# Mixed tiles of a top-k attention scaled on ScalarE and GpSimd instead of VectorE, and a re-ordered schedule

## The chip, the cores and the metric

The kernel runs on one core of a Trainium2 chip. The metric is the device time of one execution in microseconds (us), as the median of several runs.

## The reference

The reference is attention that keeps, for each query, the 32 largest of 576 scores, followed by a feed-forward block whose activation is a rational function:

```python
scores = (1 / sqrt(D)) * q @ k.transpose(0, 1, 3, 2)      # batch 8, heads 8, seq 576, D 64
kth = np.partition(scores, -32, axis=-1)[..., -32:-31]
scores = np.where(scores >= kth, scores, -1e9)
attn = exp(scores - max(scores))
attn = attn / (sum(attn) + 1e-9)
x = (attn @ v), heads side by side                        # 4608 tokens x 512
h = x @ w_in                                              # 512 -> 2048
P = a[0] + a[1]*h + a[2]*h**2 + a[3]*h**3
Q = 1 + abs(b[0])*abs(h) + abs(b[1])*h**2
out = (P / (Q + 1e-6)) @ w_out                            # 2048 -> 512
```

All data are fp32.

## The kernel before

**Tiles.** Heads are taken in pairs (hp, four pairs per batch). The 576 queries of a head are four blocks of 128 and a tail of 64. A *tile* is one head's block of 128 queries against all 576 keys; a *mixed tile* holds the 64-query tails of both heads of a pair, the one on partitions 0 to 63, the other on 64 to 127. There are 288 tiles in 160 units: 128 units of two tiles, and 32 mixed units of one.

**One tile.** TensorE makes the scores s (L570; L567 for a mixed tile), ScalarE copies them to SBUF as sb (L577). VectorE finds the 32nd largest value by folding (L596) and by rounds of MAX8 and MATCH_REPLACE8 (L602, L613, L621). GpSimd makes st, the negated maximum, ScalarE the exponentials e (L675), and VectorE the masked probabilities pr with their row sums ss (L678). The reciprocal of ss is spread over 64 columns per head as rw (`widen`, on GpSimd or ScalarE).

**One unit.** TensorE turns pr (`transpose`, L773) into a PSUM bank trp and, with the last block of keys, also rw (L775); ScalarE evacuates these as p0, p1, p2 (L785). p2 holds the last block of probabilities and, beside it, the turned reciprocals. TensorE multiplies with the values (av, L799). `scale` then multiplies av with the reciprocals. In an ordinary unit ScalarE copies av to x (L816) and GpSimd multiplies (L818). In a mixed unit VectorE does two products of 64 partitions by 64 columns, one per head (L826), into xm, which a DMA stores in xtail; the four batches of one tail chunk are fetched from there.

**Feed-forward.** The attention's output is taken in 18 chunks of 256 tokens. A chunk is split into high and low fp32r parts (xh, xl) and goes through eight groups: hidden layer (ph, 24 matmuls, L940), the rational function on ScalarE, GpSimd and VectorE (L952 to L1028), and the output product po (L1100, or L1107 for groups with split weights).

**Weights.** They come as 64-bit floating point numbers, are put together on ScalarE (L390, L401, L405), VectorE (L395) and GpSimd (L409), and are split into high and low parts (L274 on ScalarE or L276 on GpSimd, then L431) in the first 200 us, beside the attention. The keys are split the same way (L274 or L276, then L485 on GpSimd).

**The order.** All steps are entered in a list with an estimated length, a key (priority), what they depend on, and the buffers that they take and give (`add`). A planner (`Plan.run`) walks through an imagined time: an engine that is free takes the ready step with the lowest key, and a step that several engines can do goes to the first that is free. The instructions are issued in the order in which the planner starts them, and each engine runs its own in that order. The estimated lengths (`dve`, `act`, `pool_t`, ...) and the numbers in `KEY` so decide the order and the engine of every step. Buffers are rings of a few slots: two PSUM banks "mm" for trp, av and ph, one "s" for scores, one p2.

```python
bh = Hold("mm")
x = add("PE", n * pe_t, transpose(i), dep, kk, take=[bh] + ([] if at else [thold[i]]))
ev.append(add("ACT", act(n * P), evacuate(i), [x], kk + KEY['URG'], give=[bh]))
```

A second pass over everything (`full`), for data on which folding loses a value, stands behind a branch and isn't run here.

Of the kernel before, what the change touches and what calls it, by code (L numbers as in the profile page):

```python
# [10 lines left out]
F32 = mybir.dt.float32  # L11
# [6 lines left out]
AX = mybir.AxisListType  # L18
PSUM = bass.MemoryType.PSUM

KEY = {'LN': 12, 'UV': 'DVE', 'UK': -499.369, 'B0': ('ACT',), 'B1': ('POOL', 'DVE'), 'B2': ('DVE', 'POOL'), 'B3': ('DVE', 'POOL'), 'WH': ('POOL', 'ACT'), 'XH': ('POOL', 'ACT'), 'TH': 0, 'EU': -5.754, 'HW': 256, 'Q0': ('POOL', 'ACT'), 'Q1': ('POOL',), 'SPLIT': (0, 2, 4, 6), 'XS': 1, 'RH': ('ACT',), 'p2': ('POOL',), 'p4': ('POOL',), 'ratio': ('POOL',), 'ratio_low': ('POOL',), 'URG': -104.067, 'PT': -8.421, 'AV': -16.325, 'MOE': 55.665, 'LOOK': 0.27, 'T': 5.775, 'KL': -0.464, 'PJ': 35.19, 'WL': -13.886, 'EX': 43.184, 'EW': 12.91, 'ALT': {'ACT': 0.094, 'DVE': 95.307, 'POOL': 1.524}, 'WG': 4.177, 'QL': -6.4, 'PACE': 11.206, 'MS': -0.749, 'NM': ('POOL',), 'WD': ('POOL', 'ACT'), 'LP': ('POOL',), 'VL': -14.255}
NEG = -3.0e38
NB = 8

# [154 lines left out]
def tile_topk_attention__then__rational_ffn(  # L179
# [48 lines left out]
    def add(*args, **kwargs):  # L228
        return plan.add(*args, **kwargs)
# [17 lines left out]
    act = lambda n, ptr=0: 0.06 + n / 1200 + 0.094 * ptr  # L247
    act_sb = lambda n, ptr=0: act(n, ptr) + 0.04
    pool_s = lambda n, ptr=0: 0.16 + n * 0.00084 + 0.083 * ptr
    pool_t = lambda n: 0.15 + n * 0.0021  # L250
    pe_r = lambda n: max(0.109, n / 2230 + 0.003)
    pe_f = lambda n: 2 * max(0.109, n / 1200 + 0.003)
    pe_t = 0.109
# [9 lines left out]
        return {e: f[e] for e in engs}  # L263

    def fused(n, *engs):
        f = {"POOL": pool_s(n, 1) + pool_t(n), "DVE": 0.069 + n / 420}
        return {e: f[e] for e in engs}

    def engine():
# [78 lines left out]
    def weight_block(src, r0, e0, split, key, nm):  # L348
# [21 lines left out]
        else:  # L370
# [12 lines left out]
            for i in range(2):  # L383

                def low(i=i):
                    es, low, high = o.parts[i]
                    if i == 0:
                        o.bits = bank(xhold, [P, 512], f"wb_{nm}")
                        o.w = words(0) if lo is not None else hi if plain else hi(F32)
                    nc.scalar.activation(o.bits[:, es], low.bitcast(U32), AF.Identity, scale=STEP, bias=two_)  # L390

                def high(i=i):
                    es, low, high = o.parts[i]
                    x = o.bits[:, es].bitcast(I32)
# [12 lines left out]
                def join(i=i):
                    es, low, high = o.parts[i]
                    nc.gpsimd.tensor_tensor(  # L409
                        out=o.w[:, es], in0=o.w[:, es], in1=high.bitcast(F32), op=ALU.mult  # L410
                    )

                s1 = add("ACT", act(256), low, [ld] + first, key + 1,
                         take=[] if first else [xhold] + (hold if lo is not None else []))
                first = [s1]
                s2 = add("DVE", dve(256), high, [s1], key + 1)
                s3 = add("ACT", act_sb(256), sign, [s2], key + 1)
                s4 = add("ACT", act(256), size, [s2], key + 2, give=[xhold])
# [130 lines left out]
    def add_tile(t):  # L549
# [173 lines left out]
        else:  # L723
# [2 lines left out]
            a_ = add("DVE", dve(TH), best(1), [a_], key + 0.02)  # L726
            a_ = add("DVE", 0.055 + dve(TH), less(1), [a_], key + 0.04)
            a_ = add("DVE", dve(XW), best(2), [a_, b0_, b1_], key + 0.045)
            a_ = add("DVE", 0.055 + dve(XW), less(2), [a_], key + 0.046, give=[hihold])
            kb = add("DVE", dve(XW), best(3), [a_], key + 0.047)  # L730
            u.tops += [kb]
        if not full and t is u.last:
# [2 lines left out]
            u.batch.over.append(o_)  # L735
            if len(u.batch.over) == HP * NJ + HP:
                add("DVE", 0.15, worst_of(u.bi, u.batch), u.batch.over, key + 0.1, give=[u.batch.hold])
        t.probs = add("DVE", 0.06 + dve(S), probs, [kb, ex], key + 0.2, give=[sbhold, mhold, ehold])


    def add_values(u):
# [22 lines left out]
        def transpose(i):  # L764
            def emit():
# [5 lines left out]
                    cols = [slice(MAIN, MAIN + P)]  # L771
                for c, x in enumerate(cols):
                    nc.tensor.transpose(u.ps[i][:, c * P : (c + 1) * P], u.pr[:, x], ident)  # L773
                if i == 2:
                    nc.tensor.transpose(  # L775
                        u.ps[i][:, P : 2 * P], u.rw.rearrange("p h d -> p (h d)"), ident
                    )
            return emit

        def evacuate(i):  # L780
            def emit():
                n = NJ if i < 2 else 2
                if pair.pT[i] is None:
                    pair.pT[i] = buf(thold[i], [P, 2, n, P], F32, f"p{i}_{u.nm}")
                nc.scalar.copy(  # L785
                    pair.pT[i][:, at].rearrange("p c n -> p (c n)"), u.ps[i][:, 0 : n * P]
                )
            return emit

# [16 lines left out]
        def scale(part=0):  # L806
# [14 lines left out]
                return  # L821
            if not hasattr(u.batch, "xm"):
                u.batch.xm = buf("xm", [P, HP, TAIL], F32, f"xm_{u.bi}")
            for h in range(2):
                d = slice(h * D, (h + 1) * D)
                nc.vector.tensor_tensor(u.batch.xm[d, u.hp], pair.av[d, 0:TAIL], rb[d, 0, d], ALU.mult)  # L826


        def put():
            nc.sync.dma_start(u.chunk.away[:, :, u.x0 : u.x0 + TAIL], u.batch.xm)  # L830
# [7 lines left out]
        for i in ([0, 2] if u.mixed else [0, 1, 2]):  # L838
# [5 lines left out]
            bh = Hold("mm")  # L844
            n = NJ if i < 2 else 2
            kk = KEY['PT'] + (u.tiles[0].key + T if i == 0 else key + 0.4 * i)
            x = add("PE", n * pe_t, transpose(i), dep, kk, take=[bh] + ([] if at else [thold[i]]))
            tp.append(x)
            x.give = [u.phold]
            if i == 2:  # L850
                x.give = [u.phold, rwhold]
            ev.append(add("ACT", act(n * P), evacuate(i), [x], kk + KEY['URG'], give=[bh]))
            if not at:
                pair.first[i] = ev[-1]
        u.phold.users = len(tp)
# [1 line left out]
        if u is not pair.units[-1]:  # L857
            return
        avh = Hold("mm")
        n_av = 1.4 * pe_t if u.mixed else 2.7 * pe_t if lone else 4.1 * pe_t  # L860
        m = None
        cuts = [[0, 1, 2], [3, 4]] if u.mixed or lone else [[0, 1], [2, 3], [4]]
        for cs in cuts:
            m = add("PE", len(cs) * n_av, multiply(cs), [m] if m else pair.ev + [pair.vload], key + KEY['AV'],
                    take=[] if m else [avh] + ([] if u.chunk.parts or u.mixed else [u.chunk.hold]))
        m.give = [pair.vhold] + [thold[0]] + ([] if u.mixed else [thold[1]])
        m2, n = m, u.nq * len(pair.units)
# [6 lines left out]
                give=[avh, thold[2]],  # L874
            )
        else:
            s = add(
                "DVE", 2 * dve(TAIL), scale, [m2] + u.batch.xs[0:1], key + KEY['URG'],
                take=[] if u.batch.xs else [u.batch.xmhold], give=[avh, thold[2]],
            )  # L880
            u.batch.xs.append(s)
            if len(u.batch.xs) < HP:
                return
# [443 lines left out]
```

## Time and profile before

| | |
|---|---|
| median of 3 runs | 1557.52 us (1556.35 to 1557.78) |
| profiled execution: device time | 1558.06 us |
| profiled execution: span from first to last instruction | 1556.3 us |
| mean granted TensorE clock, as a share of 2.4 GHz | 0.971 |

PE is TensorE's matmuls, PEld its weight loads, DVE is VectorE, ACT ScalarE, POOL GpSimd. Busy time is the union of an engine's instructions. A matmul's duration includes its way through the array, so matmuls in a row overlap: how fast they follow each other is read from a group of several.

### The profile page before, as it was taken

The numbers are of one execution on the slowest core, as the hardware profiler recorded it, in microseconds if no ns is written. First come the engines' busy times: TensorE is split into PE (matmuls) and PEld (weight loads), VectorE is DVE, ScalarE is ACT, GpSimd is POOL, SyncE is SP. The second block draws the span as 40 slices with busy tenths as digits, with TensorE's granted clock in tenths as the row PEclk, the third lists the DMA queues.
The fourth block names the chain that finished last, engine by engine and source line by source line (L and its number), as shares of the span: only waits on it lengthen the run. The fifth ranks groups of instructions, "written<-read, shape, count | busy, mean of one in ns | idle before, by whom it ended". The sixth has DMA issues, their size and how long they took to land.

```text
span 1556.3 us, 31312 instructions
## 1 busy us (share of the span) xinstructions
PE 1431.3 (92%) x9441; PEld 1115.2 (72%) x9441; DVE 1391.3 (89%) x5541; ACT 1351.4 (87%) x2542; POOL 1155.5 (74%) x1619
## 2 busy tenths in 40 slices
PE   2447899999999999999999999999999999999996
PEld 1235666867776778777788877787787778788774
DVE  6888999999999899499999999999999989799742
ACT  6888997989898898899999998999897988798873
POOL 7877885768666795869877886688787897788520
PEclk9668999999999999999999999999999999999998
DMA  7634433233422243223422243224422333121111
GB/s 236 235 107 127 130 107 100 59 87 91 132 71 74 76 123 108 63 66 89 131 84 78 74 135 100 79 57 119 122 76 75 95 101 100 57 66 51 48 46 52
DMA packets 86802, 148.93 MB, mean 96 GB/s; under 512 B 12640, under 2 KB 38240, under 8 KB 86624
## 3 DMA queue, kind: packets, MB, share of 16 engines
q1 hardware_dynamic: 86560, 146.83, 31.5%
q8 instruction: 77, 1.26, 0.3%
q14 instruction: 101, 0.83, 0.2%
q0 software_dynamic: 64, 0.00, 0.1%
HBM read 134.22 MB, written 12.58 MB: 94 GB/s over the span
## 4 chain that ended last, share of the span: by engine, by line
PE 75%; ACT 9%; DVE 6%; POOL 4%; DMA 3%; issue 2%; SPq 1%; POOLq 0%; ACTq 0%; DVEq 0%
PE ph_m L940 20%; PE po_m L1100 12%; PE po_m L1107 11%; PE av L799 10%; PE trp L773 8%; PE s L570 7%; PE ph_t L940 3%; PE s L567 2%; ACT p L785 2%; PE po_t L1100 1%; DVE m L613 1%; PE po_t L1107 1%; ACT sb L577 1%; ACT e L675 1%; DMA out_dram<-ob_m 1%
## 5 line engine op out<-in xcount | busy, mean ns | idle before, releaser
L940 PE MATMUL ph_m<-xh_m,win_h 128*128 128x256 f32 x1024 | 314.5, 307 | 9.1 <-ACT p L785 8.5
L613 DVE MAX8 m<-x 128x8 f32<-128x192 f32 (+1 forms) x864 | 308.0, 356 | 3.4
L940 PE MATMUL ph_m<-xh_m,win_l 128*128 128x256 f32 x1024 | 287.8, 281 | 0.0
L940 PE MATMUL ph_m<-xl_m,win_h 128*128 128x256 f32 x1024 | 287.7, 281 | 0.0
L773 PE MATMUL trp<-ident,pr 128*128 128x128 f32 x1312 | 224.4, 281 | 52.1 <-ACT wout L405 17.3
L785 ACT COPY p<-trp 128x512 f32<-128x512 f32 (+1 forms) x448 | 231.2, 520 | 28.6 <-PE trp L773 20.1
L1100 PE MATMUL po_m<-wout,pa_m 128*128 128x512 f32 x512 | 247.9, 595 | 0.7 <-POOL pa_m L994 0.7
L773 PEld LDWEIGHTS trp<-ident,pr 128*128 128x128 f32 x1312 | 161.6, 143 | 119.9 <-ACT p L785 27.6
L570 PE MATMUL s<-k,q 128*128 128x288 f32 x1024 | 208.4, 327 | 37.7 <-DVE x L596 17.5
L596 DVE TENSOR_TENSOR pr<-s,sb 128x192 f32<-128x192 f32 x576 | 197.9, 345 | 49.4 <-PE trp L773 31.3
L675 ACT ACTIVATE e<-sb,st 128x576 f32<-128x576 f32 x288 | 219.2, 761 | 19.4 <-POOL st L282 14.6
L678 DVE SCALAR_TENSOR_TENSOR pr<-sb,m,e 128x576 f32<-128x576 f32 x288 | 230.2, 799 | 4.7 <-ACT e L675 2.1
L577 ACT COPY sb<-s 128x576 f32<-128x576 f32 x288 | 186.5, 647 | 50.7 <-PE s L570 37.0
L940 PEld LDWEIGHTS ph_m<-xh_m,win_h 128*128 128x128 f32 x1024 | 194.7, 190 | 27.2 <-ACT p L785 14.8
L570 PEld LDWEIGHTS s<-k,q 128*128 128x128 f32 x1024 | 154.8, 196 | 76.7 <-POOL k L485 14.0
L940 PEld LDWEIGHTS ph_m<-xl_m,win_h 128*128 128x128 f32 x1024 | 194.8, 190 | 7.2 <-issue 5.9
L602 DVE MAX8 x<-pr 128x8 f32<-128x192 f32 x576 | 198.2, 344 | 0.1
L621 DVE MATCH_REPLACE8 x<-m,x 128x192 f32<-128x192 f32 x576 | 197.4, 343 | 0.1
L940 PEld LDWEIGHTS ph_m<-xh_m,win_l 128*128 128x128 f32 x1024 | 194.0, 189 | 0.0
L799 PE MATMUL av<-p,vm 128*64 128x256 f32 (+1 forms) x1920 | 185.8, 341 | 7.7 <-ACT wout L405 3.7
L799 PEld LDWEIGHTS av<-p,vm 128*64 128x64 f32 x1920 | 110.8, 141 | 84.7 <-issue 11.6
L962 POOL TENSOR_TENSOR pa_m<-pa_m,hh_m 128x512 f32<-128x512 f32 x88 | 113.2, 1287 | 34.5 <-ACT pa_m L959 33.6
(143 smaller groups left out, 3594.9 us busy)
## 6 DMA issues: line engine op xcount, KB each, us to landing
wl_m<-wout_l SPq DMA_DIRECT2D x128, 256.0 KB, 2.7
vm<-in_v_dram SPq DMA_DIRECT2D x96, 320.0 KB, 2.9
kx<-in_qk_dram SPq DMA_DIRECT2D x32, 576.0 KB, 3.9
qx<-in_qk_dram SPq DMA_DIRECT2D x64, 256.0 KB, 2.8
km<-in_qk_dram SPq DMA_DIRECT2D x32, 352.0 KB, 3.3
w_w<-in_moe_w_out_dram SPq DMA_DIRECT2D x32, 256.0 KB, 4.0
out_dram<-ob_m SPq DMA_DIRECT2D x64, 128.0 KB, 1.7
win_h<-in_moe_w_in_dram SPq DMA_DIRECT2D x16, 256.0 KB, 6.2
```

What stands on the lines that cost most here:

```text
L570: nc.tensor.matmul(s[:, hf, 0:HF], u.pair.q.q[:, i, t.h, o : o + P], kv.k[:, t.h, cols], start=(i == 0), stop=(i == 1),)
L577: nc.scalar.copy(t.sb, t.s[:, :, 0:HF])
L596: engine().tensor_tensor(out=to, in0=one_, in1=two_, op=op)
L602: nc.vector.max(t.x[:, o : o + 8], t.w[:, 2 * i * TH :][:, 0:TH])
L613: nc.vector.max(t.m[:, 8 * r : 8 * r + 8], src)
L675: nc.scalar.activation(t.e, t.sb, AF.Exp, scale=SCALE, bias=t.st)
L678: nc.vector.scalar_tensor_tensor(out=t.pr, in0=t.sb, scalar=t.kth, in1=t.e, op0=ALU.is_ge, op1=ALU.mult, accum_out=u.ss[:, t.h : t.h + 1],)
L773: nc.tensor.transpose(u.ps[i][:, c * P : (c + 1) * P], u.pr[:, x], ident)
L785: nc.scalar.copy(pair.pT[i][:, at].rearrange("p c n -> p (c n)"), u.ps[i][:, 0 : n * P])
L799: nc.tensor.matmul(pair.av[d, 0 : u.nq * len(pair.units)], lhs, x[:, 0, d] if u.mixed else x[:, 0] if lone else x, start=(c == 0), stop=(c ...
L940: nc.tensor.matmul(y.ph[:, f * NT : (f + 1) * NT], w[c, ff][:, at : at + P], z[:, c, :], start=(c == 0 and i == 0), stop=(c == HP - 1 and ...
L1100: nc.tensor.matmul(o.po[i], y.pa[:, at], wout[ff], start=(ff == 0), stop=(ff == NF - 1),)
```

## The change

`scale` for a mixed unit is made of the two steps that an ordinary unit has: ScalarE copies av to xm (128 partitions by 64 columns), and GpSimd multiplies it in place with the reciprocals. GpSimd's operands have to lie on the same partitions and columns for both heads, so `widen` and `transpose` are changed for mixed units: the reciprocals are multiplied with a block-diagonal matrix `apart`, and a plain matmul with `fold_id` (two identities of 64, one above the other) brings those of both heads into the same 64 columns. p2 is evacuated with 192 columns instead of 256. Two constants are made at the start. Some estimated lengths of the planner are changed, and 15 numbers of `KEY`; that moves instructions on every engine.

```diff
-KEY = {... 'EU': -5.754, ... 'URG': -104.067, ... 'AV': -16.325, 'MOE': 55.665, ... 'T': 5.775, 'KL': -0.464, 'PJ': 35.19, 'WL': -13.886, 'EX': 43.184, ...}
+KEY = {... 'EU': -7.197, ... 'URG': -109.959, ... 'AV': -16.027, 'MOE': 52.047, ... 'T': 5.759, 'KL': 1.325, 'PJ': 34.509, 'WL': -12.642, 'EX': 38.379, ...}
...
-    pool_t = lambda n: 0.15 + n * 0.0021
+    pool_t = lambda n: 0.15 + n * 0.00216
...
-        f = {"POOL": pool_s(n, 1) + pool_t(n), "DVE": 0.069 + n / 420}
+        f = {"POOL": 0.12 + pool_s(n, 1) + pool_t(n), "DVE": 0.069 + n / 420}
...
+    apart = const.tile([P, P], F32, name="apart")
+    nc.gpsimd.memset(apart, 0.0)
+    for i in range(2):
+        nc.gpsimd.memset(apart[i * D : (i + 1) * D, i * D : (i + 1) * D], 1.0)
+    fold_id = const.tile([P, TAIL], F32, name="fold_id")
+    nc.scalar.copy(fold_id[0:TAIL], ident[0:TAIL, 0:TAIL])
+    nc.scalar.copy(fold_id[TAIL:P], ident[TAIL:P, TAIL:P])
...
-                s1 = add("ACT", act(256), low, [ld] + first, key + 1,
+                s1 = add("ACT", act(256) + 0.15, low, [ld] + first, key + 1,
...
-            a_ = add("DVE", 0.055 + dve(XW), less(2), [a_], key + 0.046, give=[hihold])
+            a_ = add("DVE", 0.02 + dve(XW), less(2), [a_], key + 0.046, give=[hihold])
...
-        t.probs = add("DVE", 0.06 + dve(S), probs, [kb, ex], key + 0.2, give=[sbhold, mhold, ehold])
+        t.probs = add("DVE", 0.1 + dve(S), probs, [kb, ex], key + 0.2, give=[sbhold, mhold, ehold])
...
+            if u.mixed:
+                scaled(u.rw.rearrange("p h d -> p (h d)"), apart, u.ss[:, 0:1])
+                return
...
-                if i == 2:
+                if i == 2 and u.mixed:
+                    nc.tensor.matmul(
+                        u.ps[i][:, P : P + TAIL], u.rw.rearrange("p h d -> p (h d)"), fold_id,
+                        start=True, stop=True,
+                    )
+                elif i == 2:
...
+                nw = P + TAIL if i == 2 and u.mixed else n * P
...
-                    pair.pT[i][:, at].rearrange("p c n -> p (c n)"), u.ps[i][:, 0 : n * P]
+                    pair.pT[i][:, at].rearrange("p c n -> p (c n)")[:, 0:nw], u.ps[i][:, 0:nw]
...
-            for h in range(2):
-                d = slice(h * D, (h + 1) * D)
-                nc.vector.tensor_tensor(u.batch.xm[d, u.hp], pair.av[d, 0:TAIL], rb[d, 0, d], ALU.mult)
-
+            y = u.batch.xm[:, u.hp]
+            if part == 1:
+                nc.scalar.copy(y, pair.av[:, 0:TAIL])
+            else:
+                nc.gpsimd.tensor_tensor(out=y, in0=y, in1=rb[:, 0, 0:TAIL], op=ALU.mult)
...
-            x = add("PE", n * pe_t, transpose(i), dep, kk, take=[bh] + ([] if at else [thold[i]]))
+            x = add("PE", n * (0.089 if n > 2 else 0.07), transpose(i), dep, kk, take=[bh] + ([] if at else [thold[i]]))
...
-        n_av = 1.4 * pe_t if u.mixed else 2.7 * pe_t if lone else 4.1 * pe_t
+        n_av = 0.12 if u.mixed else 0.26 if lone else 0.4
...
-            m = add("PE", len(cs) * n_av, multiply(cs), [m] if m else pair.ev + [pair.vload], key + KEY['AV'],
+            m = add("PE", 0.08 + len(cs) * n_av, multiply(cs), [m] if m else pair.ev + [pair.vload], key + KEY['AV'],
...
-            s = add(
-                "DVE", 2 * dve(TAIL), scale, [m2] + u.batch.xs[0:1], key + KEY['URG'],
-                take=[] if u.batch.xs else [u.batch.xmhold], give=[avh, thold[2]],
-            )
+            c = add("ACT", act(TAIL), lambda: scale(1), [m2] + u.batch.xs[0:1], key + KEY['URG'],
+                    take=[] if u.batch.xs else [u.batch.xmhold], give=[avh])
+            s = add("POOL", pool_t(TAIL), lambda: scale(2), [c], key + KEY['URG'], give=[thold[2]])
```

What moves is shown at two places. In the rows, q, k, kx are queries, keys and the loaded keys, win and w_w blocks of weights, wb their bits, sb the score copy, st the negated maximum; the numbers behind a name tell its block. The lines of the changed program are 7 to 16 higher than those of the kernel before.

The first place is the start, where the keys of the first tile are split. GpSimd before, from the first queries on:

```order
L276 TENSOR_SCALAR q_0_0_124<-qx_0_0_116 128x512
L518 TENSOR_TENSOR q_0_0_124<-qx_0_0_116,q_0_0_124 128x512
L276 TENSOR_SCALAR k_0_131<-kx_0_118 128x1152
L485 TENSOR_TENSOR k_0_131<-kx_0_118,k_0_131 64x1152
L409 TENSOR_TENSOR w_w_0_137<-w_w_0_137,win_h_0_120 128x256
L409 TENSOR_TENSOR w_w_0_137<-w_w_0_137,win_l_0_121 128x256
L276 TENSOR_SCALAR win_h_0_169<-w_w_0_137 128x512
```

GpSimd in the change, at the same place:

```order
L276 TENSOR_SCALAR q_0_0_131<-qx_0_0_123 128x512
L525 TENSOR_TENSOR q_0_0_131<-qx_0_0_123,q_0_0_131 128x512
L416 TENSOR_TENSOR w_w_0_139<-w_w_0_139,win_h_0_125 128x256
L416 TENSOR_TENSOR w_w_0_139<-w_w_0_139,win_l_0_126 128x256
L276 TENSOR_SCALAR win_h_0_158<-w_w_0_139 128x512
L492 TENSOR_TENSOR k_0_151<-kx_0_129,k_0_151 64x1152
```

ScalarE in the change, from the end of the first weight block to the first score copy:

```order
L412 ACTIVATE w_w_0_139<-wb_w_138 128x256
L408 ACTIVATE win_l_0_126<-win_l_0_126 128x256
L412 ACTIVATE w_w_0_139<-wb_w_138 128x256
L274 ACTIVATE k_0_151<-kx_0_129 128x1152
L397 ACTIVATE wb_w_162<-win_h_0_134,two 128x256
L397 ACTIVATE wb_w_162<-win_l_0_135,two 128x256
L408 ACTIVATE win_h_0_134<-win_h_0_134 128x256
L412 ACTIVATE w_w_0_163<-wb_w_162 128x256
L408 ACTIVATE win_l_0_135<-win_l_0_135 128x256
L412 ACTIVATE w_w_0_163<-wb_w_162 128x256
L584 COPY sb_0_0_0_184<-s_0_0_0_177 128x576
```

The high part of the first keys (`k<-kx`) has moved from GpSimd to ScalarE, behind the first weight block, and the low part on GpSimd behind that block's joins and its high part. Four steps of the second weight block (L408 and L412, L401 and L405 before) now stand ahead of the first score copy instead of behind it.

The second place is the first mixed unit. VectorE before, around its two products:

```order
L751 RECIPROCAL ss_4_1_1378<-ss_4_1_1378 128x1
L395 SCALAR_TENSOR_TENSOR wb_w_1433<-w_w_1_1355,wb_w_1433 128x256
L596 TENSOR_TENSOR x_4_2_1425<-s_4_2_0_1382,pr_4_2_1424 128x192
L826 TENSOR_TENSOR xm_1464<-av_4_0_1440,p_0_4_0_1429 64x64 x2
L602 MAX x_4_2_1425<-pr_4_2_1424 128x8
L613 MAX m_4_2_1474<-x_4_2_1425 128x8
```

ScalarE in the change, around the copy that takes their place (the row before it is the score copy of a later tile):

```order
L801 COPY p_0_4_0_1405<-trp_0_4_0_1398 128x192
L408 ACTIVATE w_w_1_1238<-w_w_1_1238 128x256
L274 ACTIVATE wout_1410<-w_w_0_1377 128x512
L412 ACTIVATE wout_1360<-wb_w_1359 128x256
L584 COPY sb_4_2_0_1424<-s_4_2_0_1365 128x576
L842 COPY xm_1435<-av_4_0_1412 128x64
L801 COPY p_0_4_1_1441<-trp_0_4_1_1428 128x512
```

GpSimd in the change, around the product:

```order
L276 TENSOR_SCALAR ss_4_1_1368<-ss_4_1_1368 128x1
L276 TENSOR_SCALAR xh_m_0_1401<-x_m_0_597 128x512
L844 TENSOR_TENSOR xm_1435<-xm_1435,p_0_4_0_1405 128x64
L919 TENSOR_TENSOR xl_m_0_1402<-x_m_0_597,xh_m_0_1401 128x512
L769 TENSOR_SCALAR pr_4_1_1318<-pr_4_1_1318 128x64
L282 TENSOR_SCALAR st_4_2_1461<-m_4_2_1460 128x1
```

The products have left VectorE's queue; a copy stands in ScalarE's, and a product in GpSimd's between the split of a chunk (xh, xl) and the doubled tail probabilities of the next mixed unit (L769).

## Rows read from the trace of the kernel before

**Rows 1.** The page, first part: busy time and share of the span by engine.

```profile
PE 1431.3 (92%) x9441; PEld 1115.2 (72%) x9441; DVE 1391.3 (89%) x5541; ACT 1351.4 (87%) x2542; POOL 1155.5 (74%) x1619
```

**Rows 2.** Windows: stretch, length; PE, PEld, DVE, ACT, POOL busy; clock, DMA share, GB/s.

```profile
0.00:200.00 200.00, 110.86 (x614) 79.21 (x616) 164.53 (x636) 164.97 (x372) 158.07 (x230) 0.82 0.51 165
200.00:596.00 396.00, 381.06 (x2578) 295.46 (x2575) 381.29 (x1563) 347.83 (x635) 294.45 (x430) 0.99 0.32 93
...
646.00:1304.00 658.00, 650.53 (x4467) 512.96 (x4464) 634.62 (x2593) 598.91 (x1106) 519.53 (x723) 1.00 0.32 92
...
1462.00:1540.00 78.00, 78.00 (x442) 60.43 (x441) 31.05 (x44) 51.28 (x87) 16.88 (x17) 1.00 0.18 55
```

**Rows 3.** Waits of TensorE, 200 to 1540 us: total us, times, longest.

```profile
PE ph_m L940 <- ACT p L785: 6.3, 7, 1.3
PE trp L773 <- ACT p L785: 5.4, 9, 1.1
PE s L570 <- DVE x L596: 3.9, 7, 1.4
...
PE trp L773 <- DVE pr L678: 1.4, 3, 0.5
```

**Rows 4.** Waits of TensorE, 0 to 200 us.

```profile
PE trp L773 <- ACT wout L405: 17.3, 6, 3.8
PE s L570 <- POOL k L485: 13.8, 1, 13.8
...
PE trp L773 <- DVE xm L826: 1.7, 2, 1.2
```

**Rows 5.** Timeline, 0 to 22 us: start, duration, engine, line, instruction.

```profile
9.88 1.15 POOL L276 TENSOR_SCALAR k<-kx 128x1152 fp32r<-128x1152 f32 x1 [0.59 <-DMA kx<-in_qk_dram]
...
11.12 2.62 POOL L485 TENSOR_TENSOR k<-kx,k 64x1152 fp32r<-64x1152 f32 x1
...
12.71 0.38 ACT L405 ACTIVATE w_w<-wb_w 128x256 f32<-128x256 f32 x1
...
13.30 0.38 ACT L405 ACTIVATE w_w<-wb_w 128x256 f32<-128x256 f32 x1
...
13.79 1.33 PE L570 MATMUL s<-k,q 128*128 128x288 f32 x4 [13.79 <-POOL k L485]
...
13.82 0.73 POOL L409 TENSOR_TENSOR w_w<-w_w,win_h 128x256 f32<-128x256 f32 x1
...
15.34 0.62 POOL L276 TENSOR_SCALAR win_h<-w_w 128x512 fp32r<-128x512 f32 x1
```

**Rows 6.** Groups of instructions by line and form: count, busy us, mean ns.

```profile
L785 ACT COPY p<-trp 128x512 f32<-128x512 f32 x288 | 170.9, 595 | 21.1 <-PE trp L773 20.1
...
L968 POOL TENSOR_TENSOR pa_m<-pa_m,h_m 128x512 f32<-128x512 f32 x88 | 113.3, 1288 | 22.3 <-ACT h_m L965 18.9 <-PE trp L773 0.8 <-POOL pa_m L962 0.2
...
L785 ACT COPY p<-trp 128x256 f32<-128x256 f32 x160 | 61.6, 385 | 7.5 <-PE trp L775 4.8 <-POOL pr L759 1.0 <-ACT p L785 0.6
...
L818 POOL TENSOR_TENSOR x_m<-x_m,p 128x256 f32<-128x256 f32 x64 | 47.6, 743 | 17.5 <-ACT x_m L816 17.0
...
L567 PE MATMUL s<-km 128*128 128x288 f32 x128 | 39.9, 436 | 1.3 <-DVE x L596 0.8 <-DMA km<-in_qk_dram 0.3
...
L274 ACT ACTIVATE k<-kx 128x1152 fp32r<-128x1152 f32 x16 | 18.7, 1170 | 0.0
...
L826 DVE TENSOR_TENSOR xm<-av,p 64x64 f32<-64x64 f32 x64 | 13.9, 218 | 1.7 <-PE av L799 0.7 <-issue 0.4
```

**Rows 7.** Timeline of TensorE, 240 to 250 us.

```profile
243.48 1.14 PE L567 MATMUL s<-km 128*128 128x288 f32 x4
...
247.10 0.60 PE L773 MATMUL trp<-ident,pr 128*128 128x128 f32 x4
...
248.39 0.27 PE L773 MATMUL trp<-ident,pr 128*128 128x128 f32 x1
```

**Rows 8.** Hidden-layer matmuls, L940: durations, first and last start.

```profile
L940 PE MATMUL ph_m<-xh_m,win_h x1024: 275/280/687, 139.1 to 1530.2; 128*128 128x256 f32 x171
```

More of the change, by code (lines that the diff above doesn't have):

```diff
@@ L19 @@
 PSUM = bass.MemoryType.PSUM
-KEY = {'LN': 12, 'UV': 'DVE', 'UK': -499.369, 'B0': ('ACT',), 'B1': ('POOL', 'DVE'), 'B2': ('DVE', 'POOL'), 'B3': ('DVE', 'POOL'), 'WH': ('POOL', 'ACT'), 'XH': ('POOL', 'ACT'), 'TH': 0, 'EU': -5.754, 'HW': 256, 'Q0': ('POOL', 'ACT'), 'Q1': ('POOL',), 'SPLIT': (0, 2, 4, 6), 'XS': 1, 'RH': ('ACT',), 'p2': ('POOL',), 'p4': ('POOL',), 'ratio': ('POOL',), 'ratio_low': ('POOL',), 'URG': -104.067, 'PT': -8.421, 'AV': -16.325, 'MOE': 55.665, 'LOOK': 0.27, 'T': 5.775, 'KL': -0.464, 'PJ': 35.19, 'WL': -13.886, 'EX': 43.184, 'EW': 12.91, 'ALT': {'ACT': 0.094, 'DVE': 95.307, 'POOL': 1.524}, 'WG': 4.177, 'QL': -6.4, 'PACE': 11.206, 'MS': -0.749, 'NM': ('POOL',), 'WD': ('POOL', 'ACT'), 'LP': ('POOL',), 'VL': -14.255}
+KEY = {'LN': 12, 'UV': 'DVE', 'UK': -499.369, 'B0': ('ACT',), 'B1': ('POOL', 'DVE'), 'B2': ('DVE', 'POOL'), 'B3': ('DVE', 'POOL'), 'WH': ('POOL', 'ACT'), 'XH': ('POOL', 'ACT'), 'TH': 0, 'EU': -7.197, 'HW': 256, 'Q0': ('POOL', 'ACT'), 'Q1': ('POOL',), 'SPLIT': (0, 2, 4, 6), 'XS': 1, 'RH': ('ACT',), 'p2': ('POOL',), 'p4': ('POOL',), 'ratio': ('POOL',), 'ratio_low': ('POOL',), 'URG': -109.959, 'PT': -8.421, 'AV': -16.027, 'MOE': 52.047, 'LOOK': 0.27, 'T': 5.759, 'KL': 1.325, 'PJ': 34.509, 'WL': -12.642, 'EX': 38.379, 'EW': 12.612, 'ALT': {'ACT': 0.094, 'DVE': 90.952, 'POOL': 1.528}, 'WG': 4.177, 'QL': -6.025, 'PACE': 11.237, 'MS': -1.055, 'NM': ('POOL',), 'WD': ('POOL', 'ACT'), 'LP': ('POOL',), 'VL': -14.255}
 NEG = -3.0e38
@@ L851, in add_values @@
                 x.give = [u.phold, rwhold]
-            ev.append(add("ACT", act(n * P), evacuate(i), [x], kk + KEY['URG'], give=[bh]))
+            ev.append(add("ACT", act(P + TAIL if i == 2 and u.mixed else n * P), evacuate(i), [x], kk + KEY['URG'], give=[bh]))
             if not at:
```

## The prediction

> **What bounds the kernel now.** I read four views. The page's first part comes first [rows 1]: TensorE is busy for 92% of the span, VectorE for 89%, ScalarE for 87%, GpSimd for 74%. With three engines that close, the average says little, so the second view cuts the span into stretches [rows 2]. The first 200 us are a stage of their own: TensorE is busy for only 110.9 us of them, at a mean granted clock of 0.82 (a mix of the two levels, 1.2 and 2.4 GHz), and no engine is above 165. From 200 to 596 us TensorE has 381.1 us of 396 and VectorE 381.3. From 646 to 1304 us TensorE has 650.5 of 658, and in the last stretch before the end, 1462 to 1540, when all scores are done and only the feed-forward part is left, 78.0 of 78.0. So from 200 us on TensorE is the engine that sets the end, and what can be had from it is its idle time: the third view, its waits, says what ends that [rows 3]. From 200 us on it names eleven pairs with 21.5 us in all: 13.1 us for ScalarE (6.3 and 5.4 for the evacuation L785, and four pairs under 1 us), 5.3 us for VectorE (3.9 and 1.4), and the rest for GpSimd and one DMA. In the first 200 us the same view [rows 4] has weight preparation on ScalarE on top (L405), the first keys on GpSimd (13.8 us, once), and 1.7 us for the VectorE product that the change removes. The fourth view is the order of time in the first 20 us [rows 5].
>
> The sum is made against the profiled execution's own 1558.06 us (span 1556.3, 1.8 around it). The median of the three runs shown, 1557.52, is 0.5 below it. About 0.2% (3.1 us) is what a measurement of this kernel can tell from no change.
>
> **The mixed tiles.** There are 32 mixed units. *VectorE* loses two 64-wide products in each: 64 by 218 ns, 13.9 us (L826) [rows 6]. *ScalarE* gains a copy of 64 columns from PSUM. No row has this size; a copy of 512 columns takes 595 ns, of 256 columns 385, so a column costs 0.82 ns and 64 columns an estimated 228 ns, 7.3 us in all (bounds: nothing, if ScalarE is idle there; 385 ns each, 12.3 us). It also evacuates 192 instead of 256 columns: 32 by 64 by 0.82 ns, 1.7 us less. *GpSimd* gains a 64-wide product: 743 ns at 256 columns and 1288 at 512 [rows 6] give 2.13 ns a column, so 334 ns, 10.7 us in all. *TensorE* turns the reciprocals with a 64-column product instead of a 128-column transpose. Four transposes last 0.60 us, one 0.27, so they follow at (0.60 - 0.27)/3 = 0.11 us [rows 7]; four plain fp32 matmuls of 288 columns last 1.14 us [rows 7] and one 0.436 [rows 6], so they follow at 0.235 us, 0.82 ns a column, and the two passes of a 64-column product take 0.10 us. That is nothing gained and nothing lost (bounds of 0.1 us a unit, 3 us either way). Of all this, only what TensorE waited for is on the path.
>
> The copy frees the PSUM bank on ScalarE instead of after two VectorE steps, and the single p2 buffer is now held until GpSimd's product. Behind that product stand the double of the next unit, then the next st, which an exponential awaits: 0.3 us of delay, and ScalarE's waits for st are not on TensorE's list. The set-up (three memsets, two copies) lies in time in which GpSimd still waits for a DMA, as it does for the first keys [rows 5]; uncovered it would cost under 1 us.
>
> **The order.** The whole changed program, counted, moves on ScalarE: 6 of the 32 key copies come to it (by 1.17 us [rows 6], 7.0) and 3 of the query copies; 6 weight copies and 3 of the x copies leave. These have 512 columns, and I take GpSimd's 0.62 us for one [rows 5]: 1.9 come, 3.7 and 1.9 go. 19 more of the 160 reciprocals' copies come too (128 columns, by the slope above 280 ns, 5.3 us). With the mixed tiles' 5.6 ScalarE has about 14 us more on 1351. VectorE stays at about 14 us less on 1391.
>
> One move I can follow exactly: the first keys. Before, GpSimd makes their high part at 9.88 us, their low part at 11.12 (2.62 us), and the first score starts at 13.79 [rows 5]. Now the high part stands on ScalarE behind the first weight block, whose last step ends there at 13.30 + 0.38 = 13.68. With 1.17 us [rows 6] it is ready at 14.8. GpSimd meanwhile takes two joins (0.73 each) and a copy (0.62) first: from 13.1, when the first join's input is ready (12.71 + 0.38), to 13.8, 14.6 and 15.2. The low part then, with the gap that separates two steps there, runs to 17.9, and the first score starts at about 18.0, 4.2 us later. ScalarE does in that time four weight steps that stood behind the first score copy before, about 0.38 us each as L405 [rows 5], so some 1.5 us comes back, and **2.7 us** stays. Bounds: 0, if the slack of the first 200 us takes it up (ScalarE is idle for 35 of them, [rows 2]), and 4.2.
>
> **What VectorE's 13.9 us are worth.** Where TensorE never waits they are worth nothing. Where it does, they are worth at most the waits: 5.3 us after 200 us [rows 3] and the 1.7 us for the product itself [rows 4], 7.0 in all. The other way: 13.9 of 1391 us is 1%, and 1% of the 396 us in which both engines are at 96% is 4.0; with the 1.7 it is 5.7. The two lie close together; the waits are measured, so I take **7.0**; bounds 0 and 13.9. ScalarE's 13.1 us of waits I leave as they are: it has more work, but in another order.
>
> **Sum:** 1558.06 + 2.7 - 7.0 = 1553.8 us, 0.24% under the median of the runs shown. Its own range, from (4.2, 3) to (0, 9), is 1549 to 1559.
>
> **The rivals.** *Hidden:* the saved VectorE time is covered by TensorE, and the first 200 us take up the late start. For it: from 646 to 1304 us TensorE lacks only 7.5 us [rows 2]. Against it: the 15 us that it lacks from 200 to 596. Between 0 and 2.7 us lost and up to 3 gained: 1557.5.
>
> *ScalarE sets the first 200 us* (the slower side). It is busy for 165 of them [rows 2], and TensorE waits 17.3 us for one kind of its weight steps alone [rows 4]. Up to the 44th score copy the changed order gives it four more key copies (4.7 us), eight scaling copies (1.8) and five more reciprocals' copies (1.4), and takes away six weight copies, two query copies and one x copy (5.6): 2.3 us more. If the late first score is not regained either: 1558.06 + 4.2 + 2.3 = 1564.6. It decides when the first hidden-layer matmul, at 139.1 us before [rows 8], starts after 143.
>
> *VectorE is the bound.* If TensorE's busy time overstates it, the removed work counts in full: 1558.06 - 13.9 + 2.7 = 1546.9. In the trace, weight loads take 1115 us, 72% of the span, under VectorE's 89% [rows 1]. Against it: between 1462 and 1540, where TensorE waits for nothing, weight loads are busy for 60.4 of 78 us, 77%, and from 646 to 1304 for 513 of 658, 78% [rows 2], so 78% is full for this mix, and TensorE is full there. The Trainium skill (Perfetto Trace Analysis, Identifying the Most-Contended Engine) says that matmul busy time is a poor measure because matmuls are pipelined, that the share of weight loads is the better one, and that the engine with the highest share is to be relieved first; by it VectorE would be that engine and this rival the forecast. The trace agrees only before 596 us, so I give it one chance in ten.
>
> **How the numbers follow.** Forecast 0.32, VectorE as the bound 0.10, hidden 0.29, ScalarE in the start 0.29. Faster is the first two, 0.42; the same 0.29; slower 0.29. The forecast leads by little: half of it rests on waits that a new order may place elsewhere. The range runs from a little under the VectorE case (the 13.9 us and no late start, 1544) to a little over the ScalarE case (1567), for the waits for ScalarE may also grow by some 2 us.
>
> **What would show it.** Right: the first score at about 18.0 us; no VectorE product for xm, copies of about 230 ns and GpSimd products of about 330 ns in its place; the first hidden-layer matmul within 3 us of 139.1; TensorE idle for about 17 us instead of 22.4 in the two stretches from 200 to 596 and 646 to 1304; its waits for VectorE near 0. Wrong: if TensorE's idle time after 200 us is as before or more, the relief is hidden or was handed to ScalarE; if it is under 10, VectorE was the bound; if the first 200 us hold more than 5 us of additional TensorE idle time, ScalarE set them.

## The result, and the profile after

The changed kernel takes **1581.72 us** (median; 1577.15 to 1584.15) against 1557.65 us for the kernel before, timed beside it: a ratio of 1.0146, 95% interval [1.0123, 1.0170]. It is 1.5% slower; the prediction said 1553.8 us and a range up to 1567. The profiled execution of the changed kernel took 1577.15 us, 19.1 more than that of before.

The page's first part, busy time and share of the span by engine:

```profile
PE 1437.6 (91%) x9473; PEld 1121.9 (71%) x9473; DVE 1385.5 (88%) x5476; ACT 1371.4 (87%) x2595; POOL 1164.0 (74%) x1639
```

Against [rows 1], VectorE has 5.8 us less, not 14, though it has 65 steps fewer, 64 of them the removed products. Its steps have not become longer: the groups by line and form add up to 11.0 us less (1734.3 instead of 1745.3). Steps that follow one another overlap, so busy time (1385.5 and 1391.3) is less than these sums, and in the change they overlap less. ScalarE has 20.0 us more for the same reason: its groups add up to only 8.2 more, where the prediction has 14. TensorE's busy time has grown by 6.3 us.

The windows of [rows 2] (stretch, length; PE, PEld, DVE, ACT, POOL busy; clock, DMA share, GB/s):

```profile
0.00:200.00 200.00, 110.22 (x582) 78.62 (x583) 155.76 (x593) 158.48 (x357) 154.55 (x233) 0.81 0.50 159
200.00:596.00 396.00, 375.77 (x2545) 292.56 (x2546) 378.30 (x1546) 355.59 (x655) 297.92 (x431) 0.99 0.32 93
646.00:1304.00 658.00, 644.40 (x4338) 505.94 (x4337) 613.88 (x2488) 600.18 (x1113) 518.00 (x712) 1.00 0.31 90
1462.00:1540.00 78.00, 78.00 (x468) 61.17 (x467) 44.30 (x118) 60.25 (x108) 29.01 (x36) 1.00 0.18 48
```

TensorE lacks 20.2 us in the second stretch (14.9 before) and 13.6 in the third (7.5 before): 33.8 us of idle time where there were 22.4, and the prediction wanted 17. In the first 200 us it is busy for 0.6 us less. The waits of TensorE from 200 to 1540 us say who ended this idle time (total us, times, longest):

```profile
PE trp L783 <- ACT p L801: 8.1, 12, 0.9
PE ph_m L956 <- ACT p L801: 7.8, 12, 1.0
PE s L577 <- DVE x L603: 5.5, 9, 1.5
PE trp L783 <- DVE pr L685: 4.9, 3, 1.6
PE trp L783 <- ACT wout L412: 1.9, 1, 1.9
PE s L577 <- ACT e L682: 1.4, 1, 1.4
```

These are the pairs of [rows 3], made longer and more frequent: the two for the evacuation p were 11.7 us in 16 waits and are 15.9 in 24; the two for VectorE were 5.3 and are 10.4. All rows of this view together are 21.5 us in 36 waits before and 33.7 in 48 after; those that ScalarE ended go from 13.1 to 21.4, those that VectorE ended from 5.3 to 11.3. So VectorE, with less work, is waited for twice as long. VectorE's own waits from 200 to 1480 us, in the changed kernel,

```profile
DVE pr L603 <- PE trp L783: 34.7, 21, 20.4
DVE pr L603 <- ACT sb L584: 18.2, 43, 1.2
DVE ss L758 <- POOL ss L276: 15.0, 35, 2.9
DVE pa_m L1035 <- ACT pa_m L975: 1.5, 2, 1.3
```

and in the kernel before:

```profile
DVE pr L596 <- PE trp L773: 26.4, 6, 19.2
DVE pa_m L1019 <- ACT pa_m L959: 12.5, 5, 5.8
DVE ss L751 <- POOL ss L276: 11.7, 25, 1.6
DVE pr L596 <- ACT sb L577: 6.4, 12, 2.1
```

Part of the time taken from VectorE became waiting of VectorE: all rows of this view are 64.2 us in 63 waits before and 73.3 in 110 after. It waits for the score copy sb on ScalarE 43 times instead of 12, 11.8 us more, and nearly as much less for pa_m on ScalarE (1.5 us instead of 12.5).

The parts that the prediction priced one by one came out as priced. The groups of the new steps (count, busy us, mean ns), which replace the L826 of [rows 6]:

```profile
L801 ACT COPY p<-trp 128x192 f32<-128x192 f32 x32 | 10.4, 324 | 3.0 <-PE trp L785 2.5
L844 POOL TENSOR_TENSOR xm<-xm,p 128x64 f32<-128x64 f32 x32 | 10.3, 323 | 10.8 <-ACT xm L842 10.7
L842 ACT COPY xm<-av 128x64 f32<-128x64 f32 x32 | 6.9, 216 | 13.9 <-PE av L815 13.7
```

The timeline of the start (start, duration, engine, line), which answers to [rows 5], has the first keys on ScalarE behind the first weight block, their low part behind GpSimd's joins, and the first score at 18.09:

```profile
13.33 0.38 ACT L412 ACTIVATE w_w<-wb_w 128x256 f32<-128x256 f32 x1
13.59 1.16 ACT L274 ACTIVATE k<-kx 128x1152 fp32r<-128x1152 f32 x1
...
15.41 2.63 POOL L492 TENSOR_TENSOR k<-kx,k 64x1152 fp32r<-64x1152 f32 x1
...
18.09 1.33 PE L577 MATMUL s<-k,q 128*128 128x288 f32 x4 [18.09 <-POOL k L492]
```

TensorE's waits in the first 200 us, which answer to [rows 4]:

```profile
PE s L577 <- POOL k L492: 18.1, 1, 18.1
PE trp L783 <- ACT w_w L412: 15.9, 6, 3.6
PE trp L783 <- ACT p L801: 11.4, 17, 0.8
PE s L577 <- DVE x L603: 9.5, 7, 2.6
PE trp L783 <- ACT wout L412: 8.0, 6, 3.8
```

The wait for the first keys has grown by 4.3 us, that for the weight step `wout` has fallen by 9.3, and none is left for xm; all rows of this view are 89.0 us before and 89.7 after. The hidden-layer matmuls, first and last start, as in [rows 8]:

```profile
L956 PE MATMUL ph_m<-xh_m,win_h x1024: 275/279/685, 143.1 to 1548.7; 128*128 128x256 f32 x171
```

Along the program, the changed kernel is 10.6 us late at the 8th tile (the start of VectorE's masked probabilities, L678 before and L685 after), 10.9 at the 64th, 9.0 at the 128th, 18.4 at the 200th and 24.0 at the last, the 288th; the last output products start 18.6 us late. That is no single place.

### The profile page after: what moved, and what is told of

Its sections match the earlier page's. It is cut to its first block, busy times and chain, and to the rows that moved or that the text cites. A ratio compares the mean times of both kernels' runs of the same rounds, so it can differ in the third digit from the quotient of the medians.

```text
span 1575.1 us, 31346 instructions
## 1 busy us (share of the span) xinstructions
PE 1437.6 (91%) x9473; PEld 1121.9 (71%) x9473; DVE 1385.5 (88%) x5476; ACT 1371.4 (87%) x2595; POOL 1164.0 (74%) x1639
## 4 chain that ended last, share of the span: by engine, by line
PE 77%; ACT 9%; DVE 6%; POOL 3%; issue 2%; DMA 2%; SPq 0%; ACTq 0%; POOLq 0%; DVEq 0%
PE ph_m L956 20%; PE po_m L1116 12%; PE po_m L1123 11%; PE av L815 11%; PE s L577 8%; PE trp L783 8%; PE s L574 2%; PE ph_t L956 2%; ACT p L801 2%; PE po_t L1116 2%; ACT sb L584 1%; DVE pr L603 1%; ACT e L682 1%; PE po_t L1123 1%; DVE m L620 1%
## 5 line engine op out<-in xcount | busy, mean ns | idle before, releaser
L956 PE MATMUL ph_m<-xh_m,win_h 128*128 128x256 f32 x1024 | 319.2, 312 | 9.8 <-ACT p L801 9.5
L956 PE MATMUL ph_m<-xl_m,win_h 128*128 128x256 f32 x1024 | 287.7, 281 | 0.0
L956 PE MATMUL ph_m<-xh_m,win_l 128*128 128x256 f32 x1024 | 287.7, 281 | 0.0
L685 DVE SCALAR_TENSOR_TENSOR pr<-sb,m,e 128x576 f32<-128x576 f32 x288 | 230.2, 799 | 3.3 <-ACT e L682 0.8
```

Of the source, the lines that this page charges most:

```text
L685: nc.vector.scalar_tensor_tensor(out=t.pr, in0=t.sb, scalar=t.kth, in1=t.e, op0=ALU.is_ge, op1=ALU.mult, accum_out=u.ss[:, t.h : t.h + 1],)
L956: nc.tensor.matmul(y.ph[:, f * NT : (f + 1) * NT], w[c, ff][:, at : at + P], z[:, c, :], start=(c == 0 and i == 0), stop=(c == HP - 1 and ...
```

## Experiments

Medians are in us; a ratio is to the kernel before, timed on the same chip in the same batch, with its 95% interval.

**Taking the change apart.** Four kernels: the mixed tiles alone, in a plan made with the numbers of before; the numbers alone; the new plan with the work of the mixed tiles back on VectorE; the new plan with its late start mended.

```diff
 # e1: the change, with KEY and the estimated lengths of before
 # e2: the kernel before, with KEY and the estimated lengths of the change
 # e3: the change; the plan is made as there, but where the copy stood VectorE
 #     does one product, and the step of GpSimd issues nothing
-            if part == 1:
-                nc.scalar.copy(y, pair.av[:, 0:TAIL])
-            else:
-                nc.gpsimd.tensor_tensor(out=y, in0=y, in1=rb[:, 0, 0:TAIL], op=ALU.mult)
+            if part == 1:
+                nc.vector.tensor_tensor(y, pair.av[:, 0:TAIL], rb[:, 0, 0:TAIL], ALU.mult)
 # e4: the change; both steps of the first keys go to GpSimd,
 #     right behind the split of the first queries
```

> The mixed tiles as in the change, all estimated lengths and numbers of KEY as in the kernel before (the planner orders the rest anew around them). Theory ORDER (the 24 us come from the re-planned order: a start that is 4 us late and then MoE and attention steps placed so that TensorE waits for evacuations): 1552 to 1562 us, first score near 13.8 us. Theory SCALARE (the copy of the mixed tiles and its place in ScalarE's queue make the evacuations late): 1572 us or more, and TensorE's waits for ScalarE's p after 200 us at 15 us or more.

> The estimated lengths and the numbers of KEY as in the change, the mixed tiles as in the kernel before (two products on VectorE). ORDER: 1575 to 1586 us, first score near 18 us. SCALARE: 1555 to 1564 us (the late start alone).

> The changed program with each instruction of every other kind in its place, but the mixed tiles scaled by one product of 128 by 64 on VectorE straight from PSUM instead of ScalarE's copy and GpSimd's product. ORDER: 1577 to 1586 us, within 4 us of the change. SCALARE: 1565 us or less.

> The changed program, but the first keys are split on GpSimd right behind the first queries, as before; the orders of TensorE, SyncE and VectorE are those of the change. Both theories: first score near 14.5 us. If the late start reaches the end: 3 to 5 us faster than the change, 1577 to 1579 us. If the first 200 us take it up: within 1.5 us of the change.

Measured: e1 1583.83, ratio 1.0163 [1.0145, 1.0182]. e2 1624.26, 1.0420 [1.0402, 1.0437]. e3 1575.08, 1.0117 [1.0083, 1.0151]. e4 1583.01, 1.0156 [1.0139, 1.0174].

In e4 the first score starts 2.15 us earlier than in the change, which the timeline of its start shows, and the median is no better than that of the change (1581.72). Whether the 2.15 us reach the end is left open by this: two executions of e4 took 1573.27 and 1575.35 us at a mean granted clock of 0.970, four 1582.39 to 1585.02 at 0.963 to 0.965; the change took 1577.15 at 0.969 and three times 1579.99 to 1584.15 at 0.964 or 0.965. In the two profiled executions e4's last output products start 3.0 us before those of the change.

```profile
12.04 1.15 POOL L489 TENSOR_SCALAR k<-kx 128x1152 fp32r<-128x1152 f32 x1 [1.94 <-DMA kx<-in_qk_dram]
13.27 2.61 POOL L491 TENSOR_TENSOR k<-kx,k 64x1152 fp32r<-64x1152 f32 x1
...
15.94 1.33 PE L594 MATMUL s<-k,q 128*128 128x288 f32 x4 [15.94 <-POOL k L491]
```

e1 shows from the other side that the late start is not the loss: it starts nearly as before (first score at 14.25, 0.4 us late at the 20th tile) and ends as late as the change. e3 keeps the change's order and takes the new work off ScalarE and GpSimd; most of the loss stays. What e1, e2 and e3 share is only that their order isn't the one of before. e1 does not separate the exchange from the order, though: the planner was given other steps with other lengths, and re-planned everything. By the expectations e1 came out as SCALARE said (TensorE's waits for p are 18.5 us there after 200 us), and ORDER missed it by 22 us; e2 lost more than either theory allowed, and e3 lies 2 us under ORDER's range and 10 over SCALARE's.

**The exchange in the old order.** So the plan was left as it was. `scale` of a mixed unit stays one step of VectorE for the planner; what is issued at its place differs. In e5 it is the change's copy and product, in e6 one VectorE product over 128 partitions; both have the change's `apart` and `fold_id`.

```diff
             y = u.batch.xm[:, u.hp]
+            # e5
+            nc.scalar.copy(y, pair.av[:, 0:TAIL])
+            nc.gpsimd.tensor_tensor(out=y, in0=y, in1=rb[:, 0, 0:TAIL], op=ALU.mult)
+            # e6
+            nc.vector.tensor_tensor(y, pair.av[:, 0:TAIL], rb[:, 0, 0:TAIL], ALU.mult)
```

> The kernel before, its planner told nothing: every instruction keeps its place, and only where a mixed unit's two VectorE products stood are ScalarE's copy and GpSimd's product issued (with the turned reciprocals of the change). Theory ORDER, sharpened after the first four runs (the exchange itself costs TensorE nothing; what costs is any new planned order, the order before being a picked one): 1552 to 1562 us. Theory SWAP (the exchange of engines costs, since the run with the mixed tiles alone lost 25 us): 1572 us or more.

> As the run before this one, but one product of 128 by 64 on VectorE in the place of two of 64 by 64, which takes some 7 us from VectorE and gives ScalarE and GpSimd nothing. ORDER: 1552 to 1560 us. SWAP: the same, since nothing is put on ScalarE.

Measured: e5 1562.62, ratio 1.0024 [1.0014, 1.0034]; e6 1557.14, 0.9986 [0.9976, 0.9996]. The page of e5, first part:

```profile
PE 1434.6 (92%) x9473; PEld 1119.9 (72%) x9473; DVE 1378.3 (88%) x5477; ACT 1354.6 (87%) x2576; POOL 1166.4 (75%) x1654
```

Its waits of TensorE from 200 to 1540 us:

```profile
PE ph_m L960 <- ACT p L800: 6.2, 7, 1.2
PE trp L782 <- ACT p L800: 5.9, 10, 1.2
PE s L576 <- DVE x L602: 1.5, 4, 0.8
```

VectorE has 13.0 us less, as priced. TensorE's wait for the folded scores falls from 3.9 to 1.5 us, the wait for the probabilities stays at 1.4, and all waits together go from 21.5 to 20.5: VectorE's relief is worth about 1 us of waiting, and the kernel is a quarter of a per cent slower. In its profiled execution 1.4 us lie in the first score, which starts at 15.21; but that moment differs by as much between kernels whose start is not touched (14.42 in e7, 15.35 in e15 below), so it proves nothing. e5's median lies 0.6 us over ORDER's range and 9 under SWAP's. e6 takes half the work off VectorE, gives none to ScalarE, and is the one version that is faster than both kernels, by 0.14%; five of its ten executions have a granted clock of 0.976 or 0.977, where the kernel before has 0.970 to 0.974, so its gain may be the clock's. Its step is this group:

```profile
L841 DVE TENSOR_TENSOR xm<-av,p 128x64 f32<-128x64 f32 x32 | 7.1, 221 | 3.8 <-PE av L814 2.6 <-issue 0.7
```

One product over 128 partitions lasts as long as one over 64, 221 against 218 ns [rows 6].

**Orders that mean nothing.** Is the order of before a picked one, so that any other loses? e7 and e15 push one key number, e9 and e13 the planner's estimate of a VectorE step by half a nanosecond; the work is the same in all.

```diff
-'T': 5.775
+'T': 5.776    # e7
+'T': 5.785    # e15
-    dve = lambda n: 0.069 + n / 960
+    dve = lambda n: 0.0695 + n / 960    # e9; in e14 the same in the change
+    dve = lambda n: 0.0685 + n / 960    # e13
```

> The kernel before with KEY's T at 5.776 instead of 5.775 and nothing else, which means nothing to the work and moves some hundred instructions by a place or more. ORDER: 1562 to 1585 us, for a new order costs even without a reason. SWAP: 1555 to 1561 us.

> The kernel before with the key number T at 5.785 instead of 5.775; about 560 of TensorE's rows change places, between the 220 of the smaller nudge (0.9996) and the 1700 of half a nanosecond (1.0203), all of them after the first 20 to 25 tiles. Theory 'the loss grows with the number of places that move': 0.4 to 1.2% slower. Rival 'the loss hangs on where, not how many': as the smaller nudge, within 0.3%, or at 1.5% and more.

> The kernel before with the planner's estimate for every VectorE step longer by 0.5 ns (0.0695 instead of 0.069 us) and nothing else. It means nothing, yet moves most of the order (some 4500 of 12300 rows of TensorE's order stand otherwise; T at 5.776 moved some 600). Theory PICKED (any thorough re-ordering costs, whatever its reason, since the order before is the best of many): 1575 to 1630 us. Theory LENGTHS (the new estimated lengths are worse ones, and the planner misplaces steps by them): 1554 to 1566 us.

> The kernel before, with the planner's estimate of a VectorE step lowered by half a nanosecond (0.0685 instead of 0.069 us); nothing else is changed, so the work is the same and about 2100 of TensorE's rows change places, a few more than with half a nanosecond added (1700 by the same count). Theory 'the order before is a picked one, and any order that differs in many places loses': 1.5 to 4% slower, as the other re-ordered programs (1.0157 to 1.042). Rival 'half a nanosecond more happened to hit a bad place, and re-orderings scatter around the time before': within 0.7% on either side of it, with an even chance of faster. Between 0.7 and 1.5%: undecided.

Measured, with the rows of TensorE that change places (matmuls in a row with the same operands are one row; the fewest of the 6145 rows in the pass that runs that have to move to make one order of the other; where an expectation has another count, it was made in another way) and all waits of TensorE from 200 to 1540 us in the profiled execution:

| | us | ratio | rows moved | waits, of these ended by ScalarE, VectorE |
|---|---|---|---|---|
| before | 1557.65 | 1 | 0 | 21.5: 13.1, 5.3 |
| e7 | 1558.66 | 0.9996 [0.9987, 1.0006] | 226 | 21.4: 15.2, 3.9 |
| e15 | 1565.48 | 1.0042 [1.0025, 1.0059] | 576 | 23.8: 16.1, 5.2 |
| e9 | 1590.86 | 1.0203 [1.0177, 1.0228] | 1256 | 36.9: 22.1, 13.3 |
| e13 | 1586.92 | 1.0176 [1.0159, 1.0193] | 1316 | 39.5: 24.4, 10.1 |
| the change | 1581.72 | 1.0146 [1.0123, 1.0170] | 1338 | 33.7: 21.4, 11.3 |

e7's push costs nothing, where ORDER expected a loss, so the order need not be exactly this one. The two that move a fifth of all rows cost 1.8 and 2.0%, on either side, and what grows are the waits that ScalarE and VectorE end, as in the change. A push also moves steps that several engines can do from one engine to another; the runs don't tell this from the order of the rows. The waits of e9, 200 to 1540 us:

```profile
PE trp L773 <- ACT p L785: 9.9, 14, 1.2
PE s L570 <- DVE x L596: 7.1, 11, 1.6
PE ph_m L940 <- ACT p L785: 6.6, 9, 1.2
PE trp L773 <- DVE pr L678: 4.2, 3, 1.6
```

The four largest are the four of the changed kernel, in a program that has none of its work.

**The new lengths and the new keys.** The change also alters eight estimated lengths; that of a GpSimd product of 512 columns goes from 1225 to 1256 ns, nearer to the 1288 of [rows 6]. e8 gives the kernel before all eight, e10 the three of TensorE, e11 the other five; e12 is the change with the KEY of before; e14 is the change with half a nanosecond added.

> The kernel before with the estimated lengths of the change and nothing else. ORDER: 1570 to 1625 us. SWAP: 1553 to 1562 us.

> The kernel before with the change's estimates for TensorE alone (transposes 0.089 or 0.07 instead of 0.109 us, the product with the values 0.4 and 0.08 instead of 0.447). LENGTHS, if they are TensorE's: 1600 to 1630 us, near the run with all new lengths. LENGTHS, if they are the others: 1554 to 1570. PICKED: 1575 to 1630, without a pattern.

> The kernel before with the change's other estimates (GpSimd's products, ScalarE's first weight step, two of VectorE's). LENGTHS, if they are TensorE's: 1554 to 1570 us. LENGTHS, if they are these: 1600 to 1630. PICKED: 1575 to 1630, without a pattern.

> The change without its numbers of KEY: mixed tiles and lengths as in the change, KEY as before. If the new numbers of KEY are what brings the change from 1624 (order alone) to 1582: 1600 us or more. If the mixed tiles do: 1575 to 1590.

> The changed kernel with the same half nanosecond added to its planner's estimate of a VectorE step; about 1500 of TensorE's rows change places. The changed kernel is 1.0146 of the kernel before; its lengths with the KEY numbers of before gave 1.0285. Theory 'the new KEY numbers were picked for the new lengths, so that a small push loses what they won': 1.022 to 1.04 of the time before. Rival 'the new lengths make a plan that is nearer to the chip and so less easily upset': 1.010 to 1.020, as the changed kernel itself.

Measured: e8 1623.79, ratio 1.0408 [1.0391, 1.0425]; e10 1598.88, 1.0270 [1.0243, 1.0296]; e11 1615.48, 1.0368 [1.0340, 1.0397]; e12 1603.51, 1.0285 [1.0259, 1.0310]; e14 1604.37, 1.0291 [1.0274, 1.0309]. All move 1370 to 1483 rows (e14 1194 against the change), and among thorough re-orderings the count tells only loosely how much is lost (e11 loses 3.7% with 1385, e14 2.9% with 1444). The new lengths make the plan worse here, not better, and each of the two parts does. All ten orders that move a fifth of the rows or more, the change's among them, lose, by 1.5 to 4.2%. From e12 to the change, which differ in KEY alone, 1.4% comes back; half a nanosecond takes it away again (e14). The numbers in KEY look as if they fit one set of lengths and one set of steps; how they were found is not known here.

## Why the prediction was wrong

**The step that failed** is the one on the order of the rest: "ScalarE's 13.1 us of waits I leave as they are: it has more work, but in another order." A re-planned order was taken as neutral. It is nearly the whole loss: the change's order loses 1.17% without the new work on ScalarE and GpSimd (e3), the exchange in the old order 0.24% (e5), the change 1.46%. Waits that ScalarE ends grow by 8.3 us and those that VectorE ends by 6.0, and an order changed by half a nanosecond does the same without the change's work (e9, e13). The notice was in the prediction ("half of it rests on waits that a new order may place elsewhere"), but the range gave it 2 us.

*The mixed tiles.* The sizes held: copy 216 ns (228 forecast), product 323 (334), VectorE 13.0 us less in the old order (13.9). *What they are worth* did not: 7.0 us in the sum; in e5, where nothing else moves, the ratio is 1.0024, a loss. The waits for VectorE were the measured ceiling, but 2.4 us of them went and the waits that ScalarE ends grew by 1.1 (13.1 to 14.2). The copies are not the reason: e6, which has none on ScalarE, has 14.2 too. This is what the rival *hidden* said, for the exchange alone.

*The start.* The time of the first score was right (18.0 forecast, 18.09 measured), its price of 2.7 us is neither shown nor refuted: e4 takes back 2.15 us of the delay, its median gains nothing, and its profiled execution is 3.0 us ahead at the end. The rival *ScalarE sets the first 200 us* met its condition narrowly (first hidden-layer matmul at 143.1 us, [rows 8] has 139.1; it asked for 143), but TensorE's idle time in the first 200 us grew by 0.6 us and not by the 5 that were to show it, and its 1564.6 came from the wrong place: e1 has the old start and the whole loss.

*VectorE is the bound* is out: e5 removes 13.0 us of VectorE and gains nothing. The Trainium skill (Perfetto Trace Analysis, Identifying the Most-Contended Engine) says to judge TensorE by its weight loads (and by its share of peak arithmetic, which no view here gives) and to relieve the engine with the highest share first; by the weight loads that is VectorE, and the measurement goes against it here. It is so from 646 to 1304 us too, where [rows 2] has 634.6 us for VectorE and 513.0 for the weight loads; the prediction saw agreement only before 596. TensorE, with 650.5 of these 658 us, is the one.

*What stays open.* Of the 19.1 us of the profiled execution, 12.2 are TensorE's waits after 200 us. About 6 are longer busy time; the page's largest group has 4.7 of it (314.5 us and a mean of 307 ns before), and the group under it is unchanged (287.7 before):

```profile
L956 PE MATMUL ph_m<-xh_m,win_h 128*128 128x256 f32 x1024 | 319.2, 312 | 9.8 <-ACT p L801 9.5 <-ACT xm L842 0.3
L956 PE MATMUL ph_m<-xl_m,win_h 128*128 128x256 f32 x1024 | 287.7, 281 | 0.0
```

Few of its matmuls are longer: the median is 280 ns in [rows 8] and 279 after. At the full clock all hidden-layer matmuls that come first behind another kind of matmul have a mean of 369 ns before and 382 after, the others 279 in both. Why is not known: it goes with the change's order (382 in e3), not with losing (368 in e9). Nor was it found which property of the order of before keeps the waits short: the runs show that the loss belongs to the order, not which rows of it. And the median of the change lies 24.1 us over that of before, 5 more than the profiled execution does over its own; the last section has what the granted clock says of that.

## What to carry to other kernels

When a program's order comes out of a planner with tuned numbers, compare a change against the kernel with the order held fixed (issue the new instructions at the place of the old ones) and against a push that means nothing; only what exceeds both is the change's. Before counting relief of an engine as gain, look at the waits that it ends on the bounding engine: 13 us less on VectorE removed 2.4 us of the waits that it ends, and 1.0 of TensorE's waits in all. A set of keys can do better with rough estimated lengths than with ones that are nearer to the trace.

## What was not expected of the hardware

A wait of TensorE can cost more than its length, by what one place shows. In the kernel before, windows of 2 us around one place (columns as above):

```profile
502.00:504.00 2.00, 1.42 (x10) 0.89 (x8) 2.00 (x10) 1.16 (x4) 2.00 (x4) 1.00 0.67 164
504.00:506.00 2.00, 0.63 (x4) 0.42 (x4) 2.00 (x10) 1.77 (x4) 1.84 (x5) 0.99 0.23 75
506.00:508.00 2.00, 1.87 (x8) 1.80 (x8) 2.00 (x8) 1.20 (x2) 2.00 (x2) 0.50 0.01 3
508.00:510.00 2.00, 1.78 (x9) 1.51 (x8) 1.72 (x8) 1.96 (x6) 1.92 (x3) 0.50 0.42 112
510.00:512.00 2.00, 2.00 (x12) 2.00 (x11) 2.00 (x10) 0.30 (x1) 1.11 (x1) 0.50 0.44 150
512.00:514.00 2.00, 2.00 (x15) 2.00 (x14) 1.47 (x6) 0.87 (x2) 0.39 (x2) 0.81 0.86 251
514.00:516.00 2.00, 2.00 (x19) 2.00 (x18) 0.46 (x2) 2.00 (x5) 0.94 (x1) 1.00 0.11 44
```

and its timeline of TensorE there:

```profile
504.09 0.63 PE L773 MATMUL trp<-ident,pr 128*128 128x128 f32 x4 [0.67 <-ACT sb L577]
506.13 1.30 PE L570 MATMUL s<-k,q 128*128 128x288 f32 x4 [1.41 <-DVE x L596]
507.22 0.41 PE L940 MATMUL ph_m<-xh_m,win_h 128*128 128x256 f32 x1
```

After waits of 0.67 and 1.41 us the granted clock falls from 1.00 to 0.50 (from 2.4 to 1.2 GHz) and stays there for 6.8 us (three windows, and 0.8 us of the next by its mean of 0.81); a hidden-layer matmul takes 0.41 us instead of 0.28. Two microseconds of waiting so cost up to 3.4 us more, an estimate: 6.8 us at half the clock. No run varied the waits of this place alone.

What the clock withheld of an execution, an upper bound of what it cost, is the span by what its mean granted clock lacks of 1. In the profiled execution of before that is 45.1 us (0.971 of 1556.3), most of it in the first 200 us, and over all executions of this kernel 40 to 47. The profiled execution of the change has 48.8 (0.969 of 1575.1), little more, but it is the shortest of four: the other three, with spans of 1577.9 to 1582.2 us at 0.964 or 0.965, have 55 to 57. In the median of the change up to about half of the loss is so the clock's, which the prediction has no term for. It goes with the order: the ten re-ordered kernels have a mean granted clock of 0.957 to 0.969 in all their executions, the kernel before, e5, e6, e7 and e15 0.969 to 0.977. In e13 it is 60.3 us (0.962 of 1587.4), 15.2 more than in the profiled execution of before, and its window from 200 to 596 us stands at 0.96, where before has 0.99 [rows 2]:

```profile
200.00:596.00 396.00, 367.68 (x2405) 286.40 (x2403) 368.15 (x1497) 340.76 (x630) 284.58 (x400) 0.96 0.29 87
```
